# Top-k attention then mixture of depths: one product in two halves, one VectorE step two maxima later

## The chip, the cores and the metric

The kernel runs on one core of one Trainium2 chip. Its time is the device time of one execution in microseconds (us), the median of several runs. The engines are called here as the profile calls them: PE is TensorE's matmul, PEld its weight load, DVE is VectorE, ACT is ScalarE, POOL is GpSimd and SP is SyncE, which issues DMAs. They run side by side, each through its own list of instructions in order, and wait for each other on semaphores.

## The reference

There are two blocks. The first is attention for 8 batches of 8 heads, 576 tokens and 64 numbers per head, in which each query keeps only the keys whose score is at least its 32nd largest. The second takes the 512 numbers of a token (8 heads side by side), scores each token with a gate vector, takes the 128 best tokens of each batch, and adds to each a small network's result, weighed by the sigmoid of the score:

```
kth = np.partition(scores, -32, axis=-1)[..., -32:-31]
scores = np.where(scores >= kth, scores, -1000000000.0)
attn = softmax(scores);  x = attn @ v          # heads side by side: x is (8, 576, 512)
s = x @ w_gate
top = argpartition(-s[b], 128)[:128]
h = maximum(x[b, top] @ w1, 0)                 # w1 is 512 x 1024
out[b, top] = x[b, top] + sigmoid(s[b, top])[:, None] * (h @ w2)   # w2 is 1024 x 512
```

## The kernel before, in words

The attention is cut into 144 units, 18 for each batch: a unit is 128 rows of queries (a tile t, of 5) for a pair of heads (a group g), with two score rows of 576 in each partition. One Python loop over n writes out a software pipeline by hand. In step n, unit n+1 gets its scores, unit n its candidates, unit n-1 its split, unit n-2 its 32nd value, unit n-3 its mask and unit n-4 its exponentials and its product with v. A wrapper (`InOrder`, line 45) keeps the instructions of each engine in the order in which the program writes them. That is why every line of the profile says L45, and why tiles' names are used to tell instructions apart.

What each engine does in a step, in order:

- PE: transposes the scores of unit n-4 into `ptr` and adds a large negative number where the mask `less` says so; turns some rows of keys and queries for the next batch; multiplies the scores `ps` of unit n+1; multiplies values `av` of unit n-4; then one piece of the mixture.
- ACT: `pT` and `last` (the exponentials of the transposed scores), the first head's mask `less`, the copy `sc` of the new scores, `xs` (the values), and `sides` of unit n-1, the sign of each score against a bound.
- DVE (`find_bound`): for each of the two rows seven maxima of eight over parts of 82 or 83 scores (`cand<-sc`); then `best` and `bound` from the candidates; then two maxima over `y` (`next<-y`), which give the 32nd value of unit n-2.
- POOL: the second head's mask `less` of unit n-3, then two products `y<-sc,sides` of unit n-1 and a small subtraction behind them, `y<-steps,seen`.

Work that comes up now and then is put on lists and run at fixed places. `vector_late` is run by `flush_vector()` inside `find_bound`, between the seven maxima of the first row and the seven of the second. It takes, among others, a reciprocal for `normalise` (whose product `x<-xs,rden` POOL makes), the mixture's comparisons `junk`, and `gates`. `gates` is one DVE instruction, `prod<-x,wg`: 512 products of a token's row with the gate vector, summed up into `gate`. It reads two tiles in SBUF, runs once for each tile t of each batch, 40 times in all, and is put last on the list, one step after POOL's `x`. For the last tile of a batch the mixture of that batch is set up right after it: SP's small DMAs `row_dram<-gate`, and POOL's split of `gate` into `parts`. The last two `gates` of the kernel are called after the loop.

The mixture is a generator that goes on by one `yield` in the steps that `mix_at` lists. Eight of its pieces are the first product (`h_ps`, 1024 x 128 out of 512), and eight the second: `y_ps`, 128 tokens by 512 columns, summed up over eight pieces of 128 rows of `w2`, one piece per step. A product in fp32 stands in the trace as two pairs of a weight load and a matmul. There are seven such mixtures; the last batch has one of its own, written out at the end, whose second product is already made in two halves of 256 columns in two PSUM banks (`av<-w,hT`).

Of the kernel before, what the change touches and what calls it, by code (L numbers as in the profile page):

```python
# [48 lines left out]
def kernel(  # L49
# [14 lines left out]
    HD = H * D  # L64
# [8 lines left out]
    NFC = F // P  # L73
# [100 lines left out]
    w2 = const.tile([P, NFC, HD], FP32, name="w2")  # L174

    def load_weights():
# [6 lines left out]
    pe, dve, act, pool, sp = (  # L183
        InOrder(tc, e)
        for e in (nc.tensor, nc.vector, nc.scalar, nc.gpsimd, nc.sync)
    )
# [14 lines left out]
        )  # L201

    late, vector_late, pool_late = [], [], []

    kept, values_bank = [], [None]

# [6 lines left out]
    def flush_vector():  # L213
        while vector_late:
            vector_late.pop(0)()
# [160 lines left out]
    def bank(pool, name, **how):  # L376
        return pool.tile([P, 512], FP32, name=name, **how)
# [101 lines left out]
    def room_for_scores():  # L479
        return ps_sc.tile([P, 2, 2, 512], FP32, name="ps")  # L480

    def room_for_first_scores():
        return [ps_first.tile([P, 2, 512], FP32, name=i) for i in ("one", "two")]
# [35 lines left out]
    def find_bound(sc, bound):  # L519

        cand = wkpool.tile([P, 2, 8 * PARTS], FP32, name="cand")
        best = [stats.tile([P, 2, 8], FP32, name=f"best{r}") for r in range(2)]
        best.append(bound)
        for i in range(2):

            if i == 1:
                flush_vector()
            for u in range(PARTS):
                dve.max(
                    cand[:, i, 8 * u : 8 * u + 8],  # L530
                    sc[:, i, u * S // PARTS : (u + 1) * S // PARTS],
                )


        parts = cand.rearrange("p i (u e) -> p i u e", u=PARTS)
        for r, e in enumerate((3, 7, 8)):
            for i in range(2):
                dve.max(best[r][:, i, :], parts[:, i, :, 0:e])
            if r < 2:
                for i in range(2):  # L540
                    dve.match_replace(
                        parts[:, i, :, 0:e],
                        best[r][:, i, :],
                        parts[:, i, :, 0:e],
                        LOWEST,
                    )
# [188 lines left out]
    def mixture(row0, pg, rank, exact=False):  # L735
# [69 lines left out]
        if exact:  # L805
            ps = ps_misc.tile([P, 512], FP32, name="place_ps", tag="misc")
        else:
            ps = values_bank[0]
        ps = ps[:, 2 * DE : 2 * DE + 6]
# [37 lines left out]
        ps = ps_misc.tile([P, 512], FP32, name="xe_ps", tag="misc")  # L847
# [7 lines left out]
        hT = modpool.tile([P, NFC, CAP], FP32, name="hT")  # L855
        for fc in range(NFC):
# [3 lines left out]
            if fc % 2 == 0:  # L860
                ps = ps_misc.tile([P, 2, CAP], FP32, name="h_ps", tag="misc")
# [8 lines left out]
        for fc in range(NFC):  # L870
            yield
            if fc == 0:
                ps = ps_misc.tile([P, 512], FP32, name="y_ps", tag="misc")
            pe.matmul(
                ps, hT[:, fc, :], w2[:, fc, :], start=(fc == 0), stop=(fc == NFC - 1)
            )
        gy = modpool.tile([P, HD], FP32, name="gy")
        late.append(
            lambda ps=ps: act.activation(gy, ps, AF.Copy, scale=g)
# [88 lines left out]
    def gates(b, t):  # L968
        dot_tile(t, *of_batch[b])

    def dot_tile(t, x, pg):
        n = R if t == J else P
        dot(n, x[0:n, t, :], pg[0][0:n, t : t + 1])
# [89 lines left out]
    def bound_of(n):  # L1063
        b, i = divmod(n, per_batch)
        if i == 0:
            bounds[b] = stats.tile([P, per_batch, 2, 8], FP32, name="bound", bufs=2)
        find_bound(scs[n], bounds[b][:, i, :, :])
# [37 lines left out]
    for n in range(-1, N):  # L1105
        b, i = divmod(n, per_batch)
# [28 lines left out]
        gating = normalised  # L1135
# [4 lines left out]
        else:  # L1140
            normalised = None
        if gating is not None:
            vector_late.append(lambda a=gating: gates(*a))

# [7 lines left out]
        if is_unit(n + 1):  # L1154
            b, t, g = units[n + 1]
            kT, qT = qkv[b][0:2]
            b, i = divmod(n, per_batch)
            if n + 1 < NHP:
                ps = room_for_first_scores()
# [4 lines left out]
            else:  # L1164
                ps = room_for_scores()
# [44 lines left out]
        if gating is not None:  # L1210
            b, t = gating
            if t == J:
                store(out[b], of_batch[b][0])
                mixtures[b] = mixture(float(b * S), of_batch[b][1], ranks[:, b, :])
        for b in mix_steps.get(n, ()):
            next(mixtures[b], None)
        b, i = divmod(n, per_batch)
# [156 lines left out]
    ps = bank(ps_end, "av3")[:, 0:6]  # L1374
# [29 lines left out]
    for dc in range(NDC):  # L1404
        at = dc % 2 * CAP
# [47 lines left out]
    hT = modpool.tile([P, NFC, CAP], FP32, name="hT")  # L1453
# [18 lines left out]
    ps = bank(ps_av, "av")  # L1472
# [11 lines left out]
    for i in range(2):  # L1484
        for fc in range(NFC):
# [4 lines left out]
                start=(fc == 0),  # L1490
                stop=(fc == NFC - 1),
# [47 lines left out]
    def general(b, row0):  # L1539
# [32 lines left out]
        for _ in mixture(row0, pg, rank, exact=True):  # L1572
            flush_all()
# [41 lines left out]
```

## Time and profile before

| what | value |
|---|---|
| time, median of 3 runs | 815.4 us (814.75 to 815.53) |
| profiled execution, its own time | 817.24 us |
| its span, first to last instruction | 815.4 us |
| DVE busy in the span | 784.2 us (96%) |
| PE / PEld busy | 777.2 (95%) / 600.3 us (74%) |
| ACT busy | 730.3 us (90%) |
| POOL busy | 721.8 us (89%) |
| `prod<-x,wg` | 40 times, 0.678 to 1.984 us, median 0.966 |
| `y_ps<-w,hT` | 112 weight loads and 112 matmuls of 128x512, 0.592 us alone |

A line of the timeline is: start, duration, engine, line, operation, tile written and tiles read, shape, how many were merged, and in brackets the idle time before it and what ended it. A line of the waits is: who waited, for whom, total us, how often, and the longest. Matmuls overlap, so a row's duration holds a tail that the next one covers.

### The profile page before, as it was taken

How to read it: one execution, taken by the hardware profiler on the slowest of the kernel's cores; microseconds unless marked ns; L12 is line 12 of the kernel's file. 1: busy time of each engine (PE TensorE's matmuls, PEld its weight loads, DVE VectorE, ACT ScalarE, POOL GpSimd, SP SyncE). 2: the span in 40 equal slices, each digit the busy share in tenths (PEclk: the TensorE clock that was granted, in tenths of full speed). 3: DMA queues.
4: the chain of work that ended last, by engine and by line, in shares of the span. 5: the costliest groups of instructions: out<-in, count | busy, mean ns of one | idle time of the engine just before them, and what ended most of it. 6: DMA issues, size and time to landing. Idle time of an engine off the chain costs nothing. (4 is left out here: it accounts for less than half of the span.)

```text
span 815.4 us, 28453 instructions
## 1 busy us (share of the span) xinstructions
PE 777.2 (95%) x10231; PEld 600.3 (74%) x10231; DVE 784.2 (96%) x4655; ACT 730.3 (90%) x1577; POOL 721.8 (89%) x722
## 2 busy tenths in 40 slices
PE   8988888888999999999999999999999999999987
PEld 6766666666887778777787777877788777867756
DVE  6999999999999999999999999999999999999962
ACT  5999999999999999999999999999999999879840
POOL 3899999999999999999999999999999999998921
PEclk9999999999999999999999999999999999999999
DMA  8931214121151223321251221512224102001021
GB/s 169 287 87 30 50 58 106 29 53 28 60 114 24 45 52 94 68 54 30 77 102 34 54 41 60 100 28 54 41 80 94 28 3 79 23 4 26 2 72 30
DMA packets 121732, 50.38 MB, mean 62 GB/s; under 512 B 116016, under 2 KB 116016, under 8 KB 120560
## 3 DMA queue, kind: packets, MB, share of 16 engines
q1 hardware_dynamic: 118368, 43.94, 21.8%
q0 software_dynamic: 1744, 4.20, 2.8%
q8 instruction: 82, 1.34, 0.7%
q14 instruction: 66, 0.54, 0.2%
q10 hardware_dynamic: 1472, 0.36, 0.2%
HBM read 36.93 MB, written 11.55 MB: 59 GB/s over the span
## 5 line engine op out<-in xcount | busy, mean ns | idle before, releaser
L45 POOL TENSOR_TENSOR y<-sc,sides 128x576 f32<-128x576 f32 x288 | 366.0, 1296 | 51.2 <-ACT sides L45 49.6
L45 DVE MAX8 cand<-sc 128x8 f32<-128x82 f32 (+1 forms) x2016 | 313.9, 227 | 4.3 <-ACT sc L45 4.3
L45 POOL TENSOR_SCALAR less<-sc,next 128x576 bf16<-128x576 f32 x135 | 233.4, 1729 | 2.9 <-DVE next L45 1.7
L45 ACT ACTIVATE sides<-sc,bound 128x576 bf16<-128x576 f32 x288 | 223.5, 790 | 0.0
L45 PE MATMUL ptr<-out_of_reach,less 128*128 128x128 bf16 x1136 | 203.3, 219 | 18.6 <-POOL less L45 18.3
L45 PE MATMUL ptr<-ident,sc 128*128 128x128 f32 x1136 | 214.6, 280 | 0.0
L45 DVE MAX8 next<-y 128x8 f32<-128x584 f32 x288 | 204.3, 751 | 0.3 <-POOL y L45 0.3
L45 PEld LDWEIGHTS av<-v,pT 128*64 128x64 f32 x4608 | 146.1, 137 | 66.1 <-ACT last L45 62.8
L45 PEld LDWEIGHTS ptr<-ident,sc 128*128 128x128 f32 x1136 | 159.8, 141 | 28.2 <-issue 16.7
L45 ACT ACTIVATE pT<-ptr 128x1024 f32<-128x1024 f32 x142 | 145.4, 1024 | 38.8 <-PE ptr L45 37.8
L45 PE MATMUL ps<-kT,qT 64*128 64x288 f32 (+1 forms) x1248 | 174.0, 425 | 0.0
L45 PE MATMUL av<-v,pT 128*64 128x65 f32 x4608 | 166.0, 224 | 8.3 <-ACT last L45 7.6
L45 PEld LDWEIGHTS <-less 128*128 128x128 bf16 x1296 | 134.4, 104 | 37.3 <-POOL less L45 24.6
L45 ACT COPY sc<-ps 128x1152 f32<-128x1152 f32 x140 | 159.1, 1137 | 0.0
L45 PEld LDWEIGHTS ps<-kT,qT 64*128 64x128 f32 (+1 forms) x1248 | 95.8, 175 | 34.5 <-issue 20.9
L45 ACT ACTIVATE less<-sc,next 128x576 bf16<-128x576 f32 x141 | 109.8, 779 | 3.6 <-DVE next L45 3.5
L45 DVE MATCH_REPLACE8 cand<-best,cand 128x21 f32<-128x21 f32 (+1 forms) x576 | 98.9, 179 | 0.0
L45 DVE MAX8 best<-cand 128x8 f32<-128x21 f32 (+1 forms) x576 | 90.3, 189 | 0.0
L45 PE MATMUL h_ps<-xeT,w 128*128 128x128 f32 x464 | 65.8, 286 | 0.0
L45 PEld LDWEIGHTS h_ps<-xeT,w 128*128 128x128 f32 x464 | 55.8, 191 | 9.1 <-issue 7.0
L45 ACT ACTIVATION_READ_ACCUMULATOR sides<-sc,bound 128x1 f32 x288 | 60.9, 211 | 0.0
L45 PE MATMUL y_ps<-w,hT 128*128 128x512 f32 x112 | 60.6, 636 | 0.0
(165 smaller groups left out, 909.3 us busy)
## 6 DMA issues: line engine op xcount, KB each, us to landing
v<-in_v_dram SPq DMA_DIRECT2D x64, 128.0 KB, 4.0
out_dram<-x SPq DMA_DIRECT2D x8, 1024.0 KB, 4.0
rows<-in_k_dram SPq DMA_DIRECT2D x56, 128.0 KB, 2.9
rows<-in_q_dram SPq DMA_DIRECT2D x56, 128.0 KB, 2.9
w<-in_moe_w_dram SPq DMA_DIRECT2D x2, 2048.0 KB, 13.9
gate_row<-row_dram SPq DMA_DIRECT2D x7, 288.0 KB, 4.3
last<-in_q_dram SPq DMA_DIRECT2D x8, 128.0 KB, 3.2
vpair<-in_v_dram SPq DMA_DIRECT2D x16, 64.0 KB, 4.3
```

Source lines behind the costliest of these rows:

```text
L45: return lambda *a, **kw: self._tc.keep_in_program_order(fn(*a, **kw))
```

## The change

The second product's pieces of the seven mixtures are made in two matmuls of 256 columns each, in place of one of 512, into the two halves of the same PSUM tile. Both halves use the same weights (`hT`), and the first half's first matmul alone opens the sum. `gates` goes on a list of its own, `amid_late`, which `find_bound` runs behind the second of the second row's seven maxima instead of ahead of the first. The last two `gates`, after the loop, and the mixture of the last batch stay as they are.

```diff
     late, vector_late, pool_late = [], [], []
+    amid_late = []
...
             if i == 1:
                 flush_vector()
             for u in range(PARTS):
+                if (i, u) == (1, 2) and amid_late:
+                    amid_late.pop()()
                 dve.max(
...
-            pe.matmul(
-                ps, hT[:, fc, :], w2[:, fc, :], start=(fc == 0), stop=(fc == NFC - 1)
-            )
+            for i in range(2):
+                at = slice(i * HD // 2, (i + 1) * HD // 2)
+                pe.matmul(
+                    ps[:, at],
+                    hT[:, fc, :],
+                    w2[:, fc, at],
+                    start=(fc == 0 and i == 0),
+                    stop=(fc == NFC - 1 and i == 1),
+                    skip_group_check=True,
+                )
...
         if gating is not None:
-            vector_late.append(lambda a=gating: gates(*a))
+            amid_late.append(lambda a=gating: gates(*a))
```

## The prediction

> **What bounds the kernel now.** I read the page's busy times first, and they mislead:
>
> ```profile
> PE 777.2 (95%) x10231; PEld 600.3 (74%) x10231; DVE 784.2 (96%) x4655; ACT 730.3 (90%) x1577; POOL 721.8 (89%) x722
> ```
>
> DVE looks like the bound, so a DVE step that gets shorter looks like time won. The waits from 300 to 700 us, the even middle of the kernel, say otherwise; these are the three longest:
>
> ```profile
> PEld av L45 <- ACT last L45: 32.5, 71, 1.1
> ACT pT L45 <- PE ptr L45: 18.4, 50, 0.7
> POOL y L45 <- ACT sides L45: 17.8, 33, 0.8
> ```
>
> The reader is to see who is missing: in these 400 us no engine waits for DVE by more than a few tenths, and DVE waits for nobody. PE waits for ACT and ACT for PE, step after step, and POOL waits for ACT. The timeline of one step shows that ring:
>
> ```profile
> 350.21 1.12 PE L45 MATMUL y_ps<-w,hT 128*128 128x512 f32 x2
> ...
> 351.17 0.27 PE L45 MATMUL ptr<-ident,sc 128*128 128x128 f32 x1
> ...
> 352.73 1.02 ACT L45 ACTIVATE pT<-ptr 128x1024 f32<-128x1024 f32 x1 [0.22 <-PE ptr L45]
> 353.65 0.27 ACT L45 ACTIVATE last<-av 128x128 f32<-128x128 f32 x1
> ...
> 354.19 1.15 PE L45 MATMUL av<-v,pT 128*64 128x65 f32 x32
> ...
> 355.50 0.70 PE L45 MATMUL y_ps<-w,hT 128*128 128x512 f32 x1
> ```
>
> Mixture product 0.96 us (350.21 to 351.17), transposes until ACT starts 1.56, the two exponentials 1.19 (to 353.92), 0.27 until the values start, values 1.31: together 5.29 us, which is the step. DVE and POOL aren't in it. The second product is.
>
> How can DVE be without idle time and yet not be the bound? Its slack is hidden inside `prod`:
>
> ```profile
> 381.07 0.98 DVE L45 CUSTOM_DVE_ANT_0 prod<-x,wg 128x512 f32<-128x512 f32 x1
> ...
> 381.46 0.67 POOL L45 TENSOR_TENSOR y<-steps,seen 128x16 f32<-128x16 f32 x1
> ```
>
> Alone a `prod` takes 0.68 us (the shortest of 40). This one met a POOL product `y` that ended at 381.50, and ended 0.55 us after it; then POOL's small subtraction took 0.67 instead of 0.22. So the two engines hold each other up: `prod` waits for the `y` in progress, and POOL's next instruction waits for `prod`. Over the 38 `prod`s in the loop the durations hold 15.9 us beyond 38 x 0.68. In a batch of 95.9 us (402.0 to 497.9, two `prod`s that stand alike) the five wait 0.78, 0.29, 0.08, 0.18 and 0.28 us, 1.6 in all. DVE could run a batch in 94.3 us; the ring needs 95.9; the waits in `prod` are where DVE loses the difference, in step with POOL.
>
> Before 200 us it is different. There PE waits for POOL's masks, and from 145 to 200 us ACT's mask waits for DVE:
>
> ```profile
> ACT less L45 <- DVE next L45: 3.5, 7, 0.7
> ```
>
> There DVE is late and does set the pace, and its `prod` runs into POOL's mask `less`:
>
> ```profile
> 168.52 1.73 POOL L45 TENSOR_SCALAR less<-sc,next 128x576 bf16<-128x576 f32 x1
> ...
> 168.70 1.11 DVE L45 CUSTOM_DVE_ANT_0 prod<-x,wg 128x512 f32<-128x512 f32 x1
> ```
>
> **The change part by part.** *The halves.* 56 pieces (7 mixtures of 8) of two load-and-matmul pairs become four pairs: 112 loads and 112 matmuls more. The last batch's own second product shows the new form, with the same operands:
>
> ```profile
> 802.99 1.24 PE L45 MATMUL av<-w,hT 128*128 128x256 f32 x5
> 803.21 0.84 PEld L45 LDWEIGHTS av<-w,hT 128*128 128x128 f32 x4
> ```
>
> Five matmuls last 1.24 us with one tail: one alone is 0.38, so they start every (1.24 - 0.38) / 4 = 0.215 us. The loads lie inside that. A piece in halves streams for 4 x 0.216 = 0.864 us. Now: eight matmuls of 512 columns at 789.98 last 3.70 us, one alone is 0.59, the first load stands 0.11 ahead (two loads that span 0.30, each 0.19): (3.70 - 0.59 - 0.11) / 7 = 0.429, so 0.858 per piece. The piece grows by 0.005 us. On the ring lie 48 pieces (five mixtures of 8 between 249 and 670 us, and 8 pieces at 713 to 732, where the step is 5.93 us and ACT waits for PE). The last mixture's 8, from 783 to 794, stand in gaps in which PE then waits for `gate`, a pick and a DMA (0.74, 0.60, 0.63 us); if that cover were gone they would cost 0.04. Sum: 48 x 0.005 = +0.25 us. Bounds: below, the same rows without taking off the lead, 4 x (7.17 - 0.38) / 31 - 2 x (3.70 - 0.59) / 7 = -0.01 per piece (-0.6 in all; 7.17 is the whole run of 32); above, both further loads exposed at 0.11 each, as the first one of a piece is, +0.22 per piece, +10.6. I take +0.25, since 31 loads in a row of the same kind show no exposure.
>
> The Trainium skill's page "TensorE: Matmul & The Clock Gate" (Part 3, the mechanism of tiling) says that a weight load overlaps a running matmul only when the two use different row groups. By that rule both further loads, 0.19 us each, would stand open: 48 x 0.38 = 18 us slower. The rows above disagree: these loads use all 128 rows and start under matmuls that do too. I go by the rows.
>
> *The gates, two maxima later.* 38 of 40 `prod`s move; each issues one DVE instruction and its accumulator read, no DMA. Seven maxima take 1.02 us from start to start (400.98 to 402.00), two take 0.29. DVE's own work doesn't change. What changes is how long a `prod` waits for POOL. Behind it on DVE now stand five maxima, `best`, `bound` and `next`; ahead of it two maxima more, which run while POOL finishes. Its readers are SP's `row_dram` DMAs and POOL's split for the last tile, at most 0.29 us later, and the first comparison that reads the gates' row comes two steps, over 10 us, after; on POOL's and SP's queues nothing changes place.
>
> In the middle: a `prod` that waits for a `y` ends 0.55 us after that `y`, whenever it began. So its end stays where it is, with two maxima already done: DVE is 0.29 us ahead after it. It reaches the next `prod` 0.29 us sooner, but behind two more maxima, so at the same moment: it waits as long as before and ends where it did. The lead stays 0.29 us and doesn't add up; POOL sees its instructions held at the same moments; the ring doesn't notice. Worth 0, covered by the ring's 1.6 us a batch. Without that cover it is worth the first rival's figure.
>
> Up to 200 us: POOL paces until the `prod` at 125.23, so the same holds, and DVE leaves it 0.29 us ahead. From there DVE is late and its lead counts. At 147.30 the ring before it is still POOL's and ACT's (ACT's mask came 0.03 us after DVE's value and hardly waited), so `prod` arrives at the same moment: nothing. At 168.70 the ring has taken over the lead of 0.3, `less` starts that much sooner, `prod` finds it 0.29 us further on, and of its wait of 0.43 (1.11 - 0.68) 0.29 goes. At 190.55 a wait of 0.14 goes, but POOL's mask at 195.86, for which PE then waits, hangs on a value found at 178, so I don't count it. Together -0.6 us, then handed on by the ring to the end. Bounds: nothing (the ring has no slack there after all), and all three waits gone with the lead, 0.29 + 0.29 + 0.29 + 0.14 = 1.0.
>
> Sum: -0.6 + 0.25 = -0.35 us. The profiled execution took 817.24 us, 1.8 beyond its span of 815.4; the span becomes 815.05. The median of the runs shown is by chance also 815.4, so 815.0 is my forecast for it. About 0.2%, 1.6 us, is what a measurement of this kernel can tell from no change; this is within it.
>
> The skill's page "SBUF — State Buffer" (Who interferes with whom) speaks against the move too: a DVE instruction with two SBUF inputs and a GpSimd instruction that reads SBUF exclude each other, and the later one waits until the earlier finishes. With `less` at 1.73 us a moved `prod` that came just behind it would wait 1.73. The trace is milder: the `prod` at 168.70 ended 0.44 us before `less` did.
>
> **Rivals.** *DVE is the bound after all.* Then each of the 38 waits shrinks by up to 0.29 us and all of it is time: summed product by product from the timeline 9.2 us, so 815.4 - 9.2 + 0.25 = 806.4. For it: DVE has no idle time. Against: nobody waits for DVE between 300 and 700 us. 0.1.
>
> *Slower: the further loads aren't hidden in the ring.* Place: each `y_ps` piece between 249 and 732 us, where the loop runs product, transposes, exponentials, values. Price +0.22 a piece, 815.4 + 10.6 - 0.6 = 825. It decides above 0.05 us a piece (2.2 / 48). For it: PE starts these steps with two kinds of work close together. Against: the rows at 803. 0.1.
>
> *Slower: `prod` slips behind POOL's `y` and into `less`.* The `prod` at 168.70 waited 0.43 with `less` 0.18 us under way, so 0.61 is the most. Five of these are 3.1 us a batch in place of 1.6; DVE would need 97.4 against the ring's 95.9, over five batches +7.5: 815.4 + 7.5 - 0.35 = 822.5. It decides when the mean wait passes 0.32. Against: the lead keeps the arrivals where they are; it needs DVE to lose its lead first. 0.07.
>
> *Neither part does anything:* 815.4, inside my forecast's case.
>
> **How the numbers follow.** My case, with the do-nothing rival, 0.63: 814 to 816.5 (the bounds -1.0 - 0.6 and +0.25 and a run's own spread of 0.4). The first rival 0.10, and 0.07 for part of it (DVE's lead counts in some batches, 811 to 813.5). The slower ones 0.17, half of that in small amounts (816.5 to 820), and 0.03 for what I don't see. So faster 0.18, same 0.62, slower 0.20. The range 812 to 818.5 leaves out most of the full rivals, under 2 in 10.
>
> **What would show it.** Right: 224 `y_ps` matmuls of 128x256 in pairs; from a piece's first load to the next transpose 0.96 to 0.97 us; the five waits of `prod` in a batch again about 1.6 us; a batch again 95.9 us; the step at 200 us some 0.6 sooner. Wrong: a batch shorter with the waits in `prod` shrunk (DVE did bind), or `ptr` starting over 1.0 us after the piece's first load, or `prod`s that end 0.44 us before a `less` in the middle.

## The result, and the profile after

The changed kernel takes 814.91 us (median of 14 runs, 814.46 to 816.77), the kernel before 815.58 (14 runs, 814.75 to 817.29): a ratio of 0.9993, 95% interval 0.9986 to 1.0000. The forecast was 815.0, the same within what can be measured. A change worth nothing would fit this time as well, so what follows rests on the traces.

The two profiled executions can be compared step by step: for the first 142 of the 144 steps (the last two transpose into other tiles) I took the start of its first transpose (`ptr<-ident,sc`) in both traces. The profiled execution of before was 1.8 us late from its very first step on, so the differences below are counted from there.

| step (time in the trace after) | after minus before, us | since the start |
|---|---|---|
| 8 to 25 (63 to 150 us) | -1.80 to -1.85 | 0 |
| 26 (155 us, behind the product at 123.4) | -2.14 | -0.3 |
| 30 (177 us, behind the product at 166.8) | -2.46 | -0.6 |
| 42 (242 us, before the first piece) | -2.45 | -0.6 |
| 86 (477 us) | -2.33 | -0.5 |
| 136 (746 us) | -2.23 | -0.4 |
| 137 to 141 | -2.13 | -0.3 |

Two steps sooner by 0.3 us, then a slow loss of 0.01 us or less per piece: -0.33 from step 8 to step 141. Behind that the trace after is another 0.3 us shorter, but so are those of `act_more` and `dve_more` below (0.27 and 0.30 us), which leave this part as it was before, so I don't count it. These are the lines of the page after, busy time first, then the three longest waits from 300 to 700 us, and the one from 145 to 200 us that set the pace there:

```profile
PE 775.4 (95%) x10343; PEld 620.0 (76%) x10343; DVE 782.7 (96%) x4655; ACT 729.6 (90%) x1577; POOL 721.7 (89%) x722
```

```profile
PEld av L45 <- ACT last L45: 32.1, 71, 1.1
ACT pT L45 <- PE ptr L45: 18.7, 50, 0.7
POOL y L45 <- ACT sides L45: 17.1, 32, 0.8
```

```profile
ACT less L45 <- DVE next L45: 2.8, 7, 0.6
```

112 more matmuls and loads, and otherwise the same picture; ACT's mask waits 0.7 us less for DVE than before. The timeline after, of the step that answers to the one shown of before:

```profile
347.82 1.13 PE L45 MATMUL y_ps<-w,hT 128*128 128x256 f32 x4
...
348.79 0.27 PE L45 MATMUL ptr<-ident,sc 128*128 128x128 f32 x1
...
350.35 1.02 ACT L45 ACTIVATE pT<-ptr 128x1024 f32<-128x1024 f32 x1 [0.23 <-PE ptr L45]
...
350.64 1.24 PE L45 MATMUL ps<-kT,qT 64*128 64x288 f32 x8
...
351.27 0.27 ACT L45 ACTIVATE last<-av 128x128 f32<-128x128 f32 x1
...
351.81 1.16 PE L45 MATMUL av<-v,pT 128*64 128x65 f32 x32
...
353.12 1.13 PE L45 MATMUL y_ps<-w,hT 128*128 128x256 f32 x4
```

The piece now takes 0.97 us (347.82 to 348.79) where it took 0.96, and the step 5.30 us where it took 5.29. Between 350.64 and 351.81 TensorE computes the next step's scores, which end as the values start: it does not wait. I had left this line out of the ring, and it matters below.

The two products whose place counted, in the timeline after: the one at 166.83 (168.70 before) now waits 0.15 us for the mask and not 0.43; one in the middle stands as before, ending 0.55 us after the `y`:

```profile
166.37 1.73 POOL L45 TENSOR_SCALAR less<-sc,next 128x576 bf16<-128x576 f32 x1
...
166.83 0.82 DVE L45 CUSTOM_DVE_ANT_0 prod<-x,wg 128x512 f32<-128x512 f32 x1
...
378.67 0.99 DVE L45 CUSTOM_DVE_ANT_0 prod<-x,wg 128x512 f32<-128x512 f32 x1
...
379.08 0.66 POOL L45 TENSOR_TENSOR y<-steps,seen 128x16 f32<-128x16 f32 x1
```

### The profile page after: what moved, and what is told of

It is laid out like the page before. It is cut to its first block, busy times and chain, and to the rows that moved or that the text cites. A ratio compares the mean times of both kernels' runs of the same rounds, so it can differ in the third digit from the quotient of the medians.

```text
span 813.0 us, 28677 instructions
## 1 busy us (share of the span) xinstructions
PE 775.4 (95%) x10343; PEld 620.0 (76%) x10343; DVE 782.7 (96%) x4655; ACT 729.6 (90%) x1577; POOL 721.7 (89%) x722
## 3 DMA queue, kind: packets, MB, share of 16 engines
q8 instruction: 83, 1.36, 0.7%
## 5 line engine op out<-in xcount | busy, mean ns | idle before, releaser
L45 PE MATMUL y_ps<-w,hT 128*128 128x256 f32 x224 | 60.9, 401 | 0.0
```

What stands on the lines that cost most here:

```text
L45: return lambda *a, **kw: self._tc.keep_in_program_order(fn(*a, **kw))
```

## The experiments

My theory was the one predicted (TensorE and ScalarE in a ring, VectorE's slack hidden in `prod`); the main rival was that VectorE binds. In the table of batches below, a batch is the time from one `prod` to the next that stands alike, and a `prod`'s wait is its duration less 0.675 us, about what the shortest one of a run takes (0.665 to 0.684).

### One part alone: the halves, and the gates

`halves_only` has the second product in halves and the gates where they were; `gates_only` the reverse.

```diff
-            pe.matmul(
-                ps, hT[:, fc, :], w2[:, fc, :], start=(fc == 0), stop=(fc == NFC - 1)
-            )
+            for i in range(2):
+                at = slice(i * HD // 2, (i + 1) * HD // 2)
...
```

```diff
-            vector_late.append(lambda a=gating: gates(*a))
+            amid_late.append(lambda a=gating: gates(*a))
```

> The second product in halves, the gates where they were. Ring theory (PE and ACT take turns and set the step from 200 us on; the further weight loads are hidden): 48 pieces on the ring at +0.005 us, +0.25 us, ratio 1.0003; from a piece's first load to the next transpose 0.97 instead of 0.96 us. Load theory (the two further loads of a piece stand open at 0.11 us each): +10 us, ratio 1.012. If the halves help for a reason that I don't see: below 1.

> The gates two maxima later, the second product whole. Ring theory: DVE gains 0.3 us at the product near 168 us and leads by 0.3 us from the one near 125 us, so -0.6 us, ratio 0.9993; from 200 to 680 us nothing, and the five products of a batch still wait about 1.6 us together. DVE theory (DVE's own list is the bound): the 38 waits shrink by 9.2 us, ratio 0.989, with about 0.5 us of waits left per batch.

Measured: `halves_only` 815.9 us against 815.45 (ratio 1.0003, 0.9994 to 1.0012); `gates_only` 814.85 against 815.45 (0.9999, 0.9989 to 1.0009). The times cannot part such small amounts, the traces can: in `halves_only` no step at 26 or 30, and a loss of 0.22 us from step 42 to step 141 (expected 0.25). In `gates_only` -0.30 at step 26, -0.30 at step 30, and 0.07 more in the steps after (expected -0.6). So the two parts are what they were taken for, and they add up to what the change shows. VectorE as the bound would have given -9; that falls.

### More cuts: four quarters

```diff
+            for i in range(4):
+                at = slice(i * HD // 4, (i + 1) * HD // 4)
+                pe.matmul(ps[:, at], hT[:, fc, :], w2[:, fc, at], ...)
```

> The second product in four matmuls of 128 columns, the gates where they were. Ring theory with hidden loads: fp32 matmuls of 128 columns start every 0.111 us in the first product's rows, so a piece streams 8 x 0.111 = 0.89 instead of 0.86 us: +0.03 on each of 48 pieces, +1.5 us, ratio 1.002. If loads of 0.19 us can't hide under matmuls of 0.11 us: 8 x 0.19 = 1.5 us per piece, +0.6, +30 us, ratio 1.037. DVE theory: nothing below +0.09 us a piece (1.6 us of slack in a batch over its eight pieces and the wait that stays).

Measured: 818.11 us (ratio 1.0037, 1.0024 to 1.0050). The part that was worked out came as said: a piece lasts 0.997 us from its first load to the next transpose (0.964 in one, 0.970 in two), +0.033, and its matmuls start 0.111 us apart, though each load takes 0.19, as the answer on the tile `y_ps` of this run says (ns: least, median, most):

```profile
L45 PEld LDWEIGHTS y_ps<-w,hT x448: 186/192/192, 247.2 to 794.4; 128*128 128x128 f32 x150
L45 PE MATMUL y_ps<-w,hT x448: 275/275/377, 247.2 to 794.6; 128*128 128x128 f32 x150
```

The skill's rule that was weighed in the prediction ("TensorE: Matmul & The Clock Gate", Part 3: a load overlaps a matmul only in another row group), taken by itself, would have added 6 loads of 0.19 to each piece; none shows. The same section also lets a load into a background weight buffer go ahead of matmuls, and these rows don't speak against that.

What was not foreseen is 0.21 us more per batch in one place, the step after the one that has no piece (it ends where steps 52, 70 and 88 start). There TensorE waits for ScalarE also in the kernel before, 0.60 us and now 0.80. The trace shows where the 0.21 comes from: in the step without a piece, ScalarE's `pT` starts 0.24 to 0.28 us after the last `ptr` ends, in each of the five batches, and not 0.04 as before. What releases it there, by the profile, is the transpose `av` that follows (in the kernel before it is `ptr`, after 0.37 us of idle time):

```profile
287.78 1.02 ACT L45 ACTIVATE pT<-ptr 128x1024 f32<-128x1024 f32 x1 [0.62 <-PE av L45]
```

Why `pT` waits for `av` there, the trace does not say.

### More work for VectorE, begun late and begun early

`dve_more` puts five maxima more (0.73 us) into the third unit of batches 2 to 6, `dve_early` four (0.58 us) into that of batches 3 to 6. Nobody reads them.

```diff
+                for _ in range(extra):
+                    spare = stats.tile([P, 8], FP32, name="spare", bufs=2)
+                    dve.max(spare, sc[:, 0, 0 : S // PARTS])
...
+        find_bound(scs[n], bounds[b][:, i, :, :], 4 if i == 2 and 3 <= b <= 6 else 0)
```

> The kernel before with five maxima more on DVE, 0.145 us each, whose results nobody reads, in the third unit of each of the batches 2 to 6: 3.6 us of DVE work more. Ring theory: they come out of the wait of the next gates' product, which is 0.78 us there and falls to about 0.05; time unchanged, ratio 1.000, and that product lasts 0.73 instead of 1.45 us. DVE theory: +3.6 us, ratio 1.0045, with the product's length unchanged or the wait moved to the following ones.

Measured: 816.84 us (ratio 1.0013, 1.0004 to 1.0022), +0.31 us a batch in the trace: neither 0 nor 3.6. The timeline of `dve_more` shows what my theory lacked:

```profile
211.32 1.73 POOL L45 TENSOR_SCALAR less<-sc,next 128x576 bf16<-128x576 f32 x1
...
211.41 1.20 DVE L45 CUSTOM_DVE_ANT_0 prod<-x,wg 128x512 f32<-128x512 f32 x1
```

This product had a wait of only 0.33 us to give (it took 1.01 in the kernel before). The 0.73 made it 0.4 late: it no longer met the `y` but the mask `less`, and waited 0.5 there. From then on, up to 671 us, every product began behind the start of the mask, and the longest waits from 300 to 700 us have a row that the kernel before does not have:

```profile
POOL less L45 <- DVE next L45: 5.4, 13, 0.6
```

So there are two states: VectorE early, held by `y` and setting nothing, or late, held by `less`, with POOL's masks waiting for it. My third rival's mechanism is real. To test that it was the state and not the work, the next run began where a product has 0.77 us to give (and it adds four maxima, not five, so the work differs a little too):

> Before with four more maxima (0.58 us of VectorE work) in the third unit of batches 3 to 6 only, 2.3 us in all: the same insertion as the one with five in batches 2 to 6, but begun where the product behind it has a wait of 0.77 us to give (in batch 2 it had only 0.33). Ring theory with two states: VectorE stays ahead; the product after the insertion falls from about 1.45 to about 0.87 us, the others stay, no product reaches POOL's mask, and the time is that of before (ratio 1.000). Late state, as in the run with five: once behind, every product meets the mask, the batch is VectorE's and grows by 0.2 us or more: +0.8 to +1.2 us (1.001 to 1.0015). VectorE binds throughout: +2.3 us (1.003).

Measured: 815.22 us against 815.21 (ratio 0.9999, 0.9990 to 1.0008), and from step 36 to the end the trace moves by 0.06 us. The product behind the insertion is exactly that much shorter (1.45 in the kernel before):

```profile
400.75 0.88 DVE L45 CUSTOM_DVE_ANT_0 prod<-x,wg 128x512 f32<-128x512 f32 x1
```

2.3 us of VectorE work cost nothing. That VectorE binds in the kernel as it stands is refuted; that it has little to spare is shown.

### Less work for TensorE

`cut` is the changed kernel with only columns 0 to 255 of the second product computed in the loop's mixtures; the other half of the row is a copy of the first.

```diff
-            for i in range(2):
+            for i in range(2 if exact else 1):
```

> The changed kernel with only the first half of the second product computed in the loop's mixtures (columns 0 to 255; the other half of the row is read from the first, so half of that product is left out). 0.43 us less TensorE work in each of the 56 pieces. Ring theory: the step shortens by 0.43 in each step with a piece, until VectorE binds, which has 0 to 1.6 us per batch to give: five batches of 0.4 to 1.6 each, and up to 8 x 0.43 = 3.4 in the last batch's pieces at 713 to 732: between 2 and 11 us faster (ratio 0.987 to 0.998), and in the middle ACT and POOL then wait for VectorE's bounds. VectorE binds already: nothing in the five batches (0.996 to 1.000).

Measured: 807.19 us (ratio 0.9908, 0.9892 to 0.9924). Every piece gives 0.43 us at first (step 43 to 46), then some of it is lost again, and the batch comes to 94.66 us in place of 95.93. Who has taken over is in the groups of TensorE over one batch, where the last column is its idle time before that group and what ended it (`cut`, 398 to 492.8 us):

```profile
L45 PE MATMUL ptr<-out_of_reach,less 128*128 128x128 bf16 x144 | 25.9, 220 | 1.1 <-POOL less L45 0.8 <-DVE less L45 0.2
L45 PE MATMUL av<-v,pT 128*64 128x65 f32 x588 | 21.3, 224 | 1.5 <-ACT last L45 1.4
```

In the changed kernel the same view of one batch (399.6 to 495.6 us) has one idle row:

```profile
L45 PE MATMUL ptr<-out_of_reach,less 128*128 128x128 bf16 x144 | 25.6, 219 | 0.0
...
L45 PE MATMUL av<-v,pT 128*64 128x65 f32 x576 | 20.8, 224 | 1.0 <-ACT last L45 1.0
```

TensorE stands still for 1.0 us of 96. It is not in turns with anyone, it is full. Take 3.4 us a batch from it and 1.3 come out before masks and exponentials are late. No run adds work to POOL; in the kernel before, TensorE waits for POOL's masks for 0.2 us between 300 and 700 us.

### Moving the piece under the exponentials

If TensorE waits for the exponentials, the piece should be done during that wait: `mid` runs it between scores and values.

```diff
+        for b in pending:
+            next(mixtures[b], None)
+        flush()
         if is_unit(n - 4):
             b4, t4, g4 = units[n - 4]
             values(t4, g4, pT, last, av, qkv[b4][2])
...
-        for b in mix_steps.get(n, ()):
-            next(mixtures[b], None)
+        pending = mix_steps.get(n, ())
```

> The changed kernel with each mixture piece moved: it runs between a step's exponentials and its values, not between the step's values and the next transposes, so TensorE does it while ScalarE makes the exponentials. If PE and ACT take turns and the piece stands on the ring, the step gets shorter by up to the piece's 0.96 us less the values' delay, capped by VectorE's 1.6 us a batch: 0.5 to 8 us faster (0.990 to 0.999), and ACT, PE or POOL wait for VectorE's values. If VectorE binds: no change (1.000). If the values, and with them the output and the next step, come later by the piece: slower.

Measured: 830.13 us (ratio 1.0182, 1.0169 to 1.0196). The timeline of `mid`:

```profile
350.94 1.24 PE L45 MATMUL ps<-kT,qT 64*128 64x288 f32 x8
...
351.74 0.27 ACT L45 ACTIVATE last<-av 128x128 f32<-128x128 f32 x1
...
352.11 1.13 PE L45 MATMUL y_ps<-w,hT 128*128 128x256 f32 x4
...
353.17 1.15 PE L45 MATMUL av<-v,pT 128*64 128x65 f32 x32
```

The last exponential ends at 352.01, and TensorE goes on from the scores to the piece at 352.11: there was no wait to fill. And the new neighbours cost: the piece takes 1.06 us behind the scores (0.97 before), the transposes 1.42 behind the values (1.36). That is 0.15 in most steps and 2.63 a batch: 98.56 us in place of 95.93. The ring as I had drawn it falls; TensorE alone fills the step (it idles 1.0 us a batch here too, for POOL's masks).

### More work for ScalarE

How far behind is ScalarE? `act_more` does the small exponential twice.

```diff
             act.activation(pT, tr, AF.Exp, scale=scale)
+            if extra:
+                act.activation(last, tr_last, AF.Exp, scale=scale)
             act.activation(last, tr_last, AF.Exp, scale=scale)
```

> Before with the small exponential, last out of av, done twice in each of the 72 steps of batches 3 to 6: 0.16 us of ScalarE work more per step, 11.8 us in all, right before the values that wait for it. PE and ACT in turns (the ring as predicted): the values start 0.16 us later in every step, +11.8 us (1.014), less only what VectorE's own limit hides. PE alone is the bound and its scores cover the exponentials (the values start 0.27 us after the last exponential ends, ScalarE waits 0.2 to 0.5 us for the transposes in two steps of three): nothing in those, up to 0.16 in the rest, 0 to +3.8 us (1.000 to 1.005).

Measured: 826.71 us (ratio 1.0139, 1.0125 to 1.0154). That is the ring's number, and by chance. The timeline of `act_more`:

```profile
359.06 0.58 ACT L45 ACTIVATE last<-av 128x128 f32<-128x128 f32 x2
...
359.69 1.15 PE L45 MATMUL av<-v,pT 128*64 128x65 f32 x32
```

The second exponential added 0.31 us and not 0.16: two take 0.58, one 0.27. The values start 0.05 us after the exponentials, where in the kernel before they start 0.27 after. So 0.22 of the 0.31 was absorbed, and the steps with a piece grow by 0.10 (5.39 for 5.29). Eleven of these make 1.05 us a batch; the four steps behind the piece-less one grow by 0.52, 0.30, 0.30 and 0.31, and one by 0.37, together the 2.85 us a batch that the trace shows. In the steps with a piece ScalarE has 0.22 us to spare; in the few around the piece-less step it has none and sets the pace: there TensorE idles 3.0 us a batch, all of it for `last`. My two cases were both too simple.

### Versions that might be faster

`gates6` is the kernel before with the gates behind the sixth maximum.

```diff
+                if (i, u) == (1, 6) and amid_late:
+                    amid_late.pop()()
```

> Before with the gates' products behind the sixth maximum and not the second, nothing else changed. Ring theory: the lead is 6 x 0.145 = 0.87 us in place of 0.29. It counts where VectorE sets the pace (the units after the products at 125 and at 168.7): about twice up to 0.6 to 0.9 us, so 1.2 to 1.8 us faster (ratio 0.998), nothing in the middle. If the lead is of no use beyond the 0.43 us that the product at 168.7 waits: 0.3 + 0.43, about 0.8 us (0.999). If the row of the gates now comes too late, or the product slips into the mask (up to 0.6 us each): slower by 1 to 5 us.

Measured: 813.84 us against 815.21 (ratio 0.9985, 0.9975 to 0.9995). In the trace -0.88 at steps 26 and 27, -0.45 at step 30, then flat: -1.2 to the end. The product at 168.75 now waits for nothing, which is why the second gain is the 0.43 that it used to wait and no more:

```profile
167.70 1.74 POOL L45 TENSOR_SCALAR less<-sc,next 128x576 bf16<-128x576 f32 x1
...
168.75 0.68 DVE L45 CUSTOM_DVE_ANT_0 prod<-x,wg 128x512 f32<-128x512 f32 x1
```

This version is faster than the kernel before, by 1.2 us in the trace, and its trace is ahead of the changed kernel's by some 0.9 us from the same start.

`between` has the gates of `gates6` and the pieces between the transposes and the scores of the next step; `spread` has them with products in halves, and moves the last half of each of four mixtures into the step that has no piece.

```diff
                 for load, half in zip(loads, halves):
                     load[0](half)
+                for m in pending:
+                    next(mixtures[m], None)
+                pending = ()
+                flush()
                 multiply(t, g, kT, qT, by_head(ps))
```

```diff
+            for i in range(2):
+                if i == 1 and fc == NFC - 1 and not exact and row0 in spread:
+                    yield
...
```

> The kernel with the gates behind the sixth maximum (products of 512 columns), and each mixture piece moved to a place between the transposes and the scores of the next step, whose neighbours in front are 128-row matmuls. PE alone is the bound: the exposed first load of a piece (0.10 us) goes and the first transpose behind the 64-column values costs 0.06 more, so -0.04 per piece, about 120 pieces: -5 us at most, and less where the later scores make ScalarE wait or VectorE binds; with the gates' -1.3 between 809 and 814 (0.993 to 0.9985). If the loads in front of the scores are exposed by 0.1 instead, as they were behind the scores when the piece was moved there: +0.06 to 0.1 per piece, +7 to +12 us (1.009 to 1.015).

> The kernel with the gates behind the sixth maximum, products in halves as in the change, and in the first four mixtures the last half product moved one step on, into the one step of the batch that has no mixture piece (4.33 us of TensorE work against 5.29). After that step TensorE now waits for ScalarE twice, 0.98 us a batch together. PE alone is the bound: up to 0.98 of gap filled, less 0.11 for one more first load, in each of four batches: 0 to -3.5 us on top of the gates' -1.3 and the halves' +0.2, so 810.5 to 814 (0.994 to 0.9987). If VectorE or ScalarE hold the batch: nothing more than the gates' share (0.9987).

Measured: `between` 817.21 us (ratio 1.0030, 1.0005 to 1.0055; its runs lie from 815.2 to 826.3, wider than any other's), `spread` 816.52 (1.0018, 1.0010 to 1.0027). In the trace of `between` each piece gains the 0.04 us worked out (a step of 5.25), a batch 0.27 of the 0.7 hoped for, and step 140, in the last batch, loses 2.75 at once, where four pieces of the last mixture's first product, and not two, are now bunched in one step. In `spread` the filled hole only moved the wait: over a batch TensorE idles 0.6 us for POOL's mask and 1.0 for ScalarE, and one product a batch is held through both `y` (2.21 us).

`both` keeps the pieces of `between` in all batches but the last, with the gates behind the sixth maximum early and behind the second later.

```diff
-        for b in mix_steps.get(n, ()):
-            next(mixtures[b], None)
+        if n < N - per_batch:
+            pending = mix_steps.get(n, ())
+        else:
+            for m in mix_steps.get(n, ()):
+                next(mixtures[m], None)
...
+        find_bound(scs[n], bounds[b][:, i, :, :], 6 if n < 40 else 2)
```

> Products of 512 columns as before; the mixture pieces between the transposes and the scores of the next step, in all batches but the last (whose pieces stay where they were, since that move cost 2.75 us at its end); the gates' products behind the sixth maximum up to the third batch and behind the second from there on. PE alone is the bound in the middle and VectorE a close second: a piece costs TensorE 0.04 to 0.05 less, 16 pieces a batch, so a batch shrinks by up to 0.7 us as long as VectorE lets it; VectorE needs 94.3 us and its waits, which were 1.36 us a batch (all behind the mask) with the gates behind the sixth maximum and should fall to about 0.4 behind the second, where a product begins before the mask does. So a batch between 94.9 and 95.3 in place of 95.93 over five batches: -3 to -5 us, with the gates' lead early on, -1.3: 809.5 to 811.5 (0.993 to 0.995). If the waits behind the mask stay: 95.65 a batch, 812.5 to 813 (0.997). If ScalarE, which gets its scores 0.3 us later, holds the steps: no better than the gates alone (0.9985).

Measured: 821.4 us (ratio 1.0075, 1.0061 to 1.0089), worse than any case of mine. The products did leave the mask, and fell into the second `y` instead. They stand there in the kernel before too, but in four of five with 0.1 to 0.3 us to wait; here each of the five waits 0.38 to 0.75. This is the timeline of `both`, and TensorE's group over its batch:

```profile
432.45 2.52 POOL L45 TENSOR_TENSOR y<-sc,sides 128x576 f32<-128x576 f32 x2
...
434.14 1.38 DVE L45 CUSTOM_DVE_ANT_0 prod<-x,wg 128x512 f32<-128x512 f32 x1
```

```profile
L45 PE MATMUL ptr<-out_of_reach,less 128*128 128x128 bf16 x144 | 26.0, 220 | 1.9 <-POOL less L45 1.9
```

TensorE now waits for POOL's masks. The batch is 97.33 us, in a part of the kernel in which TensorE works 95.4. Why VectorE and POOL settle in this order and not in that of `cut`, I can't say; I had worked out one place of the products and not where they move to once the batch shortens.

### All batches side by side

| kernel | a batch, us | waits in its five `prod`s | batch less waits |
|---|---|---|---|
| before | 95.92 | 1.61 | 94.31 |
| after | 95.93 | 1.65 | 94.28 |
| `gates6` | 95.92 | 1.66 | 94.26 |
| `dve_early` | 95.94 | 1.05 | 94.89, with 0.58 added |
| `dve_more` | 96.23 | 1.21 | 95.02, with 0.73 added |
| `quarters` | 96.42 | 2.12 | 94.30 |
| `cut` | 94.66 | 0.38 | 94.28 |
| `between` | 95.66 | 1.36 | 94.30 |
| `spread` | 96.59 | 2.31 | 94.28 |
| `both` | 97.33 | 3.05 | 94.28 |
| `mid` | 98.56 | 4.26 | 94.30 |
| `act_more` | 98.77 | 1.96 | 96.81 |

Less the added work, the last column is the same in every row but the last, whether TensorE binds (`mid`) or TensorE waits for the masks (`both`): in these runs VectorE shows no idle time, so its waits inside `prod` are simply what is left of the batch. In `act_more`, where ScalarE sets the pace in some steps, VectorE does show idle time, 1.5 us a batch in gaps over 0.15 us, and the column is 2.5 larger. Where there is no idle time, the sum of the waits says how much VectorE has to spare if it is early, and says nothing about who binds. Only the other engines' waits do.

## Why the prediction was right, and where it was not

- **The halves, +0.25 us.** Right. 0.005 us a piece; +0.22 in `halves_only`. The rival with exposed loads (+10) is out.
- **The gates, -0.6 us before 200 us, from the products at 125 and 168.7.** Right in place and size: -0.30 and -0.30 in the change and in `gates_only`. The wait of 0.14 at 190.55 went (0.67 us now) and gave nothing, as said.
- **Nothing in the middle.** Right: five waits of 1.65 us against 1.61, a batch of 95.93 against 95.92, and the lead of 0.29 did not add up. What covers it is TensorE's full list, not the ring that I named.
- **"PE and ACT take turns."** Wrong as a mechanism. The step that failed is the sum "the two exponentials 1.19, 0.27 until the values start": in those 1.46 us TensorE is not waiting but moving rows and computing scores. The row that misled me is the longest wait from 300 to 700 us, 32.5 us of `av` for `last`. It belongs to the queue of weight loads, which waits while the matmuls ahead of it run. TensorE itself idles 0.9 us a batch in the kernel before. The conclusion that the second product stands on the path held all the same, since a piece on a full TensorE is on the path too. TensorE's own row for the same wait stands further down in the same view of the kernel before, and is a tenth as long:

```profile
PE av L45 <- ACT last L45: 3.2, 8, 0.6
```

- **VectorE is the bound (chance 0.1).** Refuted by `gates_only` and `dve_early`. It comes next, with ScalarE, when TensorE gets 1.3 us a batch shorter (`cut`).
- **`prod` into the mask (chance 0.07).** It did not happen in the change. "It needs DVE to lose its lead first" is what `dve_more` did with 0.4 us, at 0.3 us a batch and not the 1.5 that I priced: the waits on the mask came to 1.21 us a batch, not 3.1.
- **Not foreseen:** the 0.10 us at step 137, which neither `halves_only` nor `gates_only` shows. There the product started between POOL's two `y` and not during the first; it took 0.67 us and not 1.77, and the second `y` was held instead, the two taking 3.06 us where they usually take 2.52:

```profile
742.47 3.06 POOL L45 TENSOR_TENSOR y<-sc,sides 128x576 f32<-128x576 f32 x2
...
743.72 0.67 DVE L45 CUSTOM_DVE_ANT_0 prod<-x,wg 128x512 f32<-128x512 f32 x1
```

## What to carry to other kernels

Before a wait is called part of the bound, ask what the engine itself does meanwhile: a wait on the weight-load queue under running matmuls is no idle time, and the groups of one batch with their idle column settle it in one look. An engine without idle time may still have slack, inside instructions that are held by another engine; to find out, add work right before such an instruction, little enough that it stays in the order it had. Where engines stand within a few per cent of each other, a move that is free in its place can change the order in which they meet elsewhere: price the order that comes after, or expect a loss.

## What the runs showed that I had not expected

- VectorE's product and POOL's work hold each other in both directions. In `cut` the product started 0.04 us ahead of the mask, and the mask took 2.22 us in place of 1.72. That is milder than what the skill's page "SBUF — State Buffer" (Who interferes with whom) says, that the later of the two waits until the earlier is done: 0.63 us of the product were left when the mask began, and it lost 0.50:

```profile
398.09 0.67 DVE L45 CUSTOM_DVE_ANT_0 prod<-x,wg 128x512 f32<-128x512 f32 x1
...
398.13 2.22 POOL L45 TENSOR_SCALAR less<-sc,next 128x576 bf16<-128x576 f32 x1
```

- An exponential done twice into the same tile costs 0.31 us more, though `less` starts 0.16 us after `last` does.
- Where a group of matmuls stands costs more than how finely it is cut: behind the scores a piece takes 1.06 us, behind the values 0.97, behind the transposes 0.95, and the transposes 1.42 behind the values and 1.36 behind a piece; cutting it in two costs 0.005.
